# A fused attention and feed-forward block: a weight load moved to ScalarE's queue, another held back, and new instruction orders

## The chip, the cores and the metric

The kernel runs on one core of a Trainium2 chip. The metric is device time in microseconds (us) of one launch; the median of three runs before the change is 183.61 us (183.45 to 183.64). Engines: TensorE (PE in the profile, with its weight loads as PEld), VectorE (DVE), ScalarE (ACT), GpSimd (POOL) and SyncE (SP). Before the change every transfer is issued from SP's queue.

## The reference

With `xn = layernorm(x)` for 2048 rows of 512 features, the result is `x + A(xn) + B(xn)`, all in bf16:

```python
qkv = (xn @ wqkv)                      # 512 -> 3 x 512, 32 heads of 16
# A: row s attends to rows s, s-2, ..., s-14 (8 offsets), masked below row 0
logits = einsum("bhsd,bhswd->bhsw", q, k[idx]) / 4
A = (softmax(logits) @ v[idx]) @ wo    # 512 -> 512
# B: gated feed-forward
B = (gelu(xn @ w_gate) * (xn @ w_up)) @ w_down   # 512 -> 1376 -> 512
```

## The kernel before, in words

**Tiling.** The rows are cut into four blocks b = 0 to 3 of 512 rows, sixteen tiles of 128. For each block the kernel normalizes the rows, brings them into transposed form `xnT`, makes q, k and v, the eight logits of each head, a softmax, the weighted sum of v, the feed-forward products, and one output product that adds both branches in the same PSUM bank. The blocks overlap: while VectorE is at the attention of one block, TensorE is at the feed-forward of the same or the next.

**Tasks and names.** Each piece of work is a named task of one engine, with the line on which its instruction stands in the profile of before. The name ends in the block, and after that in the part; `fu0_3` is the fourth up-projection of block 0. For block 0 and the head of the program the last number is a tile.

- TensorE: `warm` (L637, products of constants while x is on its way), `tpx0_t`, `tpy0_t` (L883, the two halves of the transpose of tile t = 0, 1), `tpx1_t` (L872, tiles 2 and 3), `mma0_t`, `mmb0_t` (L961, q of tile t from the first and the second half of the features), `mmt0_t`, `mmt1_t` (L947, q of tiles 2, 3 and k of all four), `mmv` (L1005, v of block 0), `fg`, `fu` (L1250, gate and up; part 10 on L1289), `mmB_w_g_0` (L1030, q, k, v for w = 0, 1, 2 of blocks 1 to 3), `er` (L1097 the last piece of the up-projection, then L1104 the sum over a head's features), `acca`, `accb`, `accd`, `accw` (L1342, the output product).
- VectorE: `bnst`, `bnag`, `sub`, `rstd`, `norm` (L712 to L842, layernorm of tiles 0 to 7; `rstd8` to `rstd14` on L765), `mean1`, `evy0_t` (L897, half of a transposed tile out of PSUM), `pr` (L1061, q times eight shifted k), `pa`, `pb` (L1073, L1080, sums of these), `mask` (L1127), `d1`, `d2` (L1138, L1145, the maximum and its subtraction), `d4` (L1164), `d6` (L1182), `pv` (L1212, weights times shifted v), `pw`, `pz` (L1221 to L1232, their sums), `h` (L1274, L1312, gate times up), `fin` (L1380, L1386, adding x).
- ScalarE: `c_tbl` (L627, a one-element square root that brings in its table), `sx1`, `negm1`, `sxx1`, `sq` (L722 to L768, the statistics of tile 1 and the square roots), `evx0_t`, `evx1_t` (L905), `evq`, `evk`, `evv` (L983, L1015, L1041), `gelu`, `uev` (L1260, L1267), `bnst8` to `15`, `bnag8` to `15`, `sub8` to `15`, `norm8` to `15` (the layernorm of the later tiles), `ve`, `vp`, `va` (L762), `vb` (L790), `lc` (L1133), `exp`, `ln`, `d5` (L1156, L1174, L1178), `halo`, `halv` (L1049), `fe` (L1375).
- GpSimd: constants, and `sq8`, `sq10`, `sq12`, `sq14` (L794, a power of one half of two columns, between `vb` and `rstd`).
- SP's queue: `ld_x` (L693, L699), `ld_wq`, `ld_wk`, `ld_wv` (L646), `ld_wg0`, `ld_wu0` (L655), `ld_wt` (L662), `ld_wd` (L667, L671), `ld_wo` (L674), `trx` (L855, transposes of tiles 4 to 15 into `xnT`, two numbers: pair of tiles and tile of the pair), `ss` and `sl` (L1191, L1204, the softmax weights through memory and back, spread), `ldxr` (L1327, x again for `fin`), `sto` (L1393, the result).

**What sets the order.** The table `ORDER` holds, written out, one list of task names for each engine, and every engine runs its list strictly in turn. `Graph.schedule` walks the five lists with a table of costs (durations, `nbytes` for a load) to see which buffer slot each task gets; the same walk gives `assign_sync` the waits: a task waits for the semaphores of what it depends on. So the costs in the tasks do not move an instruction past another on its engine; they can only change which slot is taken and which wait is found to be covered by an earlier one. A list entry with `on_act` set is issued by ScalarE's queue, ahead of all of ScalarE's own tasks.

**Buffers around the change.** `XIN` has four slots for pairs of tiles of x. In the order of before x0, x1, x2 and x4 take the four; `ld_x3` stands behind them, and waits for the slot of x0, which is free when `tpy0_1` has read tile 1. `ld_wg0` depends on `ld_wk` having landed. `XR` has two slots for `ldxr0` to `ldxr7`; a third load waits for the `fin` of an earlier one. `xnT` of a block is complete when its four `trx` have landed, and the block's `mm` wait for all four.

Of the kernel before, what the change touches and what calls it, by code (L numbers as in the profile page):

```python
# [96 lines left out]
class Graph:  # L97
# [225 lines left out]
    def emit_engine(self, eng_name, e):  # L323
        if eng_name == "act":
            for t in self.order["sp"]:
                if t.on_act:
                    assert not t.waits
                    ins = t.emit(e)
                    ins.then_inc(t.sem, 16)
                    t.ins_name = ins.ins.name  # L330
# [17 lines left out]
    def report(self):  # L348
# [17 lines left out]
        "warm13 warm14 mma0_0 tpx0_1 tpy0_1 mmb0_0 mma0_1 mmb0_1 mmt1_0 tpx1_0 mmt1_1 mmt0_2 tpx1_1 mmt1_2 "  # L366
        "mmv0_1 mmt0_3 mmt1_3 mmv0_0 mmv1_0 fg0_0 fg0_1 fg0_2 fg0_3 fu0_0 fu0_1 fu0_2 fu0_3 fg0_4 mm1_0_0_0 "
        "fu0_4 mm1_1_0_0 fg0_5 mm1_1_1_0 fu0_5 er0_3 mm1_0_1_0 fg0_6 mm1_2_3_0 fg1_0 mm1_0_2_0 mm1_1_2_0 "
        "mm1_0_3_0 mm1_1_3_0 fu1_0 fg0_7 fu0_6 fu0_7 fg1_1 fu1_1 fg0_10 fg0_8 fg1_2 fu1_2 fg1_3 mm1_2_2_0 "
        "fu1_3 fg0_9 fg1_4 mmv1_1 fu1_4 fu0_8 fu0_9 er1_3 fg1_5 mm1_2_0_0 fg1_6 fu1_5 fg1_7 fg1_8 fu1_6 fg1_9 "  # L370
        "fu1_7 mm2_1_0_0 mm2_0_0_0 mm2_1_3_0 fu1_8 mm2_1_1_0 mm2_0_2_0 fg2_0 mm2_0_1_0 mm1_2_1_0 mm2_0_3_0 "
        "fu2_0 mm2_1_2_0 fg1_10 accd3 fu1_9 fg2_1 fu2_1 fg2_2 fg2_3 fg2_4 mm2_2_2_0 acca0 fu2_2 accb0 fg2_5 "
        "accd1 fg2_10 er2_3 fg2_6 mm2_2_3_0 mm2_2_1_0 mm2_2_0_0 mm3_0_2_0 mm3_0_3_0 fu2_3 fu2_4 mm3_1_1_0 "
        "mm3_1_2_0 fu2_5 accd2 mm3_0_0_0 mm3_1_3_0 fg3_0 mm3_1_0_0 fu2_6 fg3_1 fu3_0 fg2_7 fu3_1 fg3_2 "
        "mm3_0_1_0 fg3_3 mm3_2_2_0 fu3_2 mm3_2_0_0 acca4 fu3_3 fu2_7 accd7 accd5 er3_3 fg2_8 accb4 fg3_4 "
        "fg3_5 fg2_9 fu2_8 mm3_2_1_0 accd6 fg3_6 mm3_2_3_0 fu3_4 fu3_5 fg3_7 fg3_8 fu2_9 fg3_10 fu3_6 fu3_7 "
        "fg3_9 fu3_8 fu3_9 acca8 accb8 accd11 acca12 accd15_1 accd9 accb12 accd13 accd14_0 accd10 accd15_0 "
        "accw13 accw15_1 accw15_0 accw12 accd14_1 accw14_0 accw14_1 accd15_2 accw15_2",
    "act":
        "c_tbl sx1 sq0 negm1 sxx1 sq1 evx0_0 evx0_1 sq2 evq0_0 evq0_1 evx1_0 sq3 evk0_0 evk0_1 bnst8 evx1_1 "  # L380
        "bnst9 sq4 evk0_2 ve8 sq6 evq0_2 vp8 evq0_3 evk0_3 bnag8 evv0_0_1 bnag9 evv0_1_0 sub9 gelu0_0 bnst10 "
        "bnst11 uev0_0 va8 gelu0_3 gelu0_1 ve10 gelu0_2 vp10 evv0_0_0 uev0_3 vb8 evq1_0_0 bnag10 evk1_0_0 "
        "uev0_4 uev0_2 bnag11 uev0_1 va10 halo1 bnst12 evk1_1_0 vb10 lc0 evq1_1_0 uev0_5 gelu0_5 gelu0_6 "
        "gelu0_4 exp0 evq1_2_0 evv1_3_0 evq1_3_0 bnst13 evk1_3_0 ln0 d5_0 evk1_2_0 gelu1_0 sub10 uev0_6 "
        "gelu1_1 uev1_1 uev1_0 sub8 uev0_10c ve12 uev0_10a uev0_10b uev0_7 norm8 gelu0_10 gelu0_8 sub11 "
        "gelu0_7 evv1_2_0 gelu1_3 gelu1_2 vp12 uev1_2 evv0_1_1 uev1_3 gelu1_4 norm11 uev0_9 uev0_8 lc1 bnag12 "
        "norm10 gelu0_9 norm9 gelu1_6 uev1_4 bnag13 evv1_0_0 uev1_5 bnst14 gelu1_7 uev1_6 gelu1_5 bnst15 "
        "uev1_7 gelu1_8 gelu1_9 exp1 evk2_1_0 uev1_8 evq2_0_0 va12 ve14 evk2_0_0 halo2 vb12 sub13 vp14 halv1 "
        "evv1_1_0 evq2_1_0 evk2_3_0 bnag14 uev1_10b sub12 ln1 d5_1 uev1_10c evk2_2_0 evq2_3_0 uev1_10a "
# [48 lines left out]
def bass_parallel_sum__sliding_local_dilated__glu_gated_geglu__prompt_kernel(nc, A_x, A_wqkv, A_wo, B_x, B_w_gate, B_w_up, B_w_down, out, dbg=None, cfg=None):  # L438
# [43 lines left out]
    with contextlib.ExitStack() as es:  # L482
# [61 lines left out]
        G = Graph()  # L544
# [912 lines left out]
```

## Time and profile before

| | us |
|---|---|
| median of three runs (range) | 183.61 (183.45 to 183.64) |
| the profiled execution | 183.42 |
| its span, first to last instruction | 181.3 |
| PE, DVE, ACT, POOL busy | 176.5, 168.7, 131.7, 18.5 |
| first `warm` product, first transpose, first product with Wq | 0.83, 4.93, 5.94 |
| first gate product `fg0_0` | 16.74 |
| last product ends | 178.98 |

The timeline gives start and duration of an instruction or of a run of like ones; the second figure of a run of matmuls contains the modelled drain of the last, so that runs overlap by some 0.17 us. The step from one start to the next is the time that a task takes of the stream. `SPq` is the issue of a transfer on SP's queue. The waits view sums the idle time of an engine by what ended it. What lies between the span and the profiled time (2.1 us) is before the first and after the last instruction.

### The profile page before, as it was taken

How to read it: one execution, taken by the hardware profiler on the slowest of the kernel's cores; microseconds unless marked ns; L12 is line 12 of the kernel's file. 1: busy time of each engine (PE TensorE's matmuls, PEld its weight loads, DVE VectorE, ACT ScalarE, POOL GpSimd, SP SyncE). 2: the span in 40 equal slices, each digit the busy share in tenths (PEclk: the TensorE clock that was granted, in tenths of full speed). 3: DMA queues.
4: the chain of work that ended last, by engine and by line, in shares of the span. 5: the costliest groups of instructions: out<-in, count | busy, mean ns of one | idle time of the engine just before them, and what ended most of it. 6: DMA issues, size and time to landing. Idle time of an engine off the chain costs nothing.

```text
span 181.3 us, 2762 instructions
## 1 busy us (share of the span) xinstructions
PE 176.5 (97%) x1043; PEld 90.7 (50%) x1060; DVE 168.7 (93%) x157; ACT 131.7 (73%) x270; POOL 18.5 (10%) x23
## 2 busy tenths in 40 slices
PE   8999999999999999999999999999999999999994
PEld 2897444544454455444445444444444444454574
DVE  3989996899999999989999999999999999999953
ACT  5689999999999999999297599835177679411030
POOL 6000035200000002954000000000000000000000
PEclk9999999999999999999999999999999999999999
DMA  4999984002792200002671000518004057410113
GB/s 130 357 379 386 156 218 162 2 0 58 161 329 56 58 4 0 0 0 66 168 206 29 0 0 0 140 61 266 29 0 147 3 120 226 146 58 4 58 47 98
DMA packets 26220, 19.60 MB, mean 108 GB/s; under 512 B 13824, under 2 KB 23008, under 8 KB 26208
## 3 DMA queue, kind: packets, MB, share of 16 engines
q1 hardware_dynamic: 26208, 19.44, 38.1%
q8 instruction: 8, 0.13, 0.3%
q14 instruction: 4, 0.03, 0.1%
HBM read 14.71 MB, written 3.15 MB: 98 GB/s over the span
## 4 chain that ended last, share of the span: by engine, by line
DVE 54%; ACT 21%; PE 10%; POOL 5%; DMA 5%; issue 4%; SPq 1%; DVEq 0%
DVE UNI L1212 14%; DVE UNI L1061 9%; DVE UNI L1221 7%; POOL sq L794 5%; ACT GG L1260 4%; DVE UNI L1073 4%; ACT UU L1267 4%; DVE UNI L1227 4%; DVE HT L1274 3%; DMA XIN<-in_A_x_dram 3%; PE PS L1342 3%; PE PS L637 2%; DVE OT L1232 2%; DVE OB L1380 2%; DMA xnT<-XIN 2%
## 5 line engine op out<-in xcount | busy, mean ns | idle before, releaser
L1342 PE MATMUL PS<-Wd,HT 128*128 128x512 bf16 (+2 forms) x206 | 40.5, 345 | 0.2
L1250 PE MATMUL PS<-xnT,Wu 128*128 128x512 bf16 x156 | 38.9, 379 | 0.2
L1250 PE MATMUL PS<-xnT,Wg 128*128 128x512 bf16 x155 | 38.7, 379 | 0.4 <-issue 0.2
L1212 DVE TENSOR_TENSOR UNI<-VN,PT 128x8192 f16<-128x8192 bf16 x8 | 35.4, 4420 | 0.0
L1061 DVE TENSOR_TENSOR UNI<-QT,KT 128x8192 f16<-128x8192 bf16 x8 | 35.3, 4420 | 0.0
L1030 PE MATMUL PS<-xnT,Wqkv 128*128 128x512 bf16 x142 | 34.5, 380 | 0.3
L1342 PEld LDWEIGHTS PS<-Wd,HT 128*128 128x128 bf16 x209 | 19.7, 98 | 19.4
L1267 ACT ACTIVATE UU<-PS 128x512 bf16<-128x512 f32 x40 | 23.2, 608 | 6.0 <-PE PS L1250 5.9
L1375 ACT ACTIVATE OB<-PS 128x512 bf16<-128x512 f32 x14 | 8.3, 595 | 23.2 <-PE PS L1342 23.1
L1250 PEld LDWEIGHTS PS<-xnT,Wu 128*128 128x128 bf16 x160 | 15.6, 98 | 18.6 <-ACT KT L1041 0.3
L1250 PEld LDWEIGHTS PS<-xnT,Wg 128*128 128x128 bf16 x160 | 15.1, 98 | 19.4 <-ACT UU L1267 0.8
L1030 PEld LDWEIGHTS PS<-xnT,Wqkv 128*128 128x128 bf16 x144 | 16.1, 114 | 16.0 <-DMA xnT<-XIN 0.6
L1260 ACT ACTIVATE GG<-PS 128x512 bf16<-128x512 f32 x40 | 22.9, 609 | 0.5 <-DVE HT L1274 0.4
L794 POOL TENSOR_TENSOR sq<-ve,mhalf 128x2 bf16<-128x2 f32 x4 | 15.7, 3916 | 65.8 <-ACT ve L790 65.8
L1221 DVE TENSOR_TENSOR UNI<-UNI 128x8192 f16<-128x8192 f16 x4 | 17.7, 4422 | 0.0
L1073 DVE TENSOR_TENSOR UNI<-UNI 128x8192 f16<-128x8192 f16 x4 | 17.7, 4421 | 0.0
L1342 PE MATMUL PS<-Wo,OT 128*128 128x512 bf16 (+2 forms) x75 | 16.1, 345 | 0.1
L1274 DVE TENSOR_TENSOR HT<-GG,UU 128x1024 bf16<-128x1024 bf16 x20 | 13.5, 685 | 0.0
L1342 PEld LDWEIGHTS PS<-Wo,OT 128*128 128x128 bf16 x76 | 6.9, 98 | 6.4 <-DVE OT L1232 0.5
L1227 DVE TENSOR_TENSOR UNI<-UNI 128x4096 f16<-128x4096 f16 x4 | 9.1, 2286 | 0.0
L1041 ACT ACTIVATE KT<-PS 128x512 bf16<-128x512 f32 x12 | 7.2, 600 | 2.4 <-PE PS L1030 2.4
L1041 ACT ACTIVATE VN<-PS 128x512 bf16<-128x512 f32 x12 | 7.2, 598 | 1.0 <-PE PS L1030 0.9
(99 smaller groups left out, 180.3 us busy)
## 6 DMA issues: line engine op xcount, KB each, us to landing
PT<-pt_scratch SPq DMA_DIRECT2D x16, 256.0 KB, 4.3
out_dram<-OB SPq DMA_DIRECT2D x14, 128.0 KB, 1.8
XIN<-in_A_x_dram SPq DMA_DIRECT2D x12, 128.0 KB, 2.6
Wqkv<-in_A_wqkv_dram SPq DMA_DIRECT2D x3, 512.0 KB, 5.0
XIN<-in_A_x_dram SPq DMA_DIRECT2D x6, 256.0 KB, 5.8
Wg<-in_B_w_gate_dram SPq DMA_DIRECT2D x1, 1280.0 KB, 8.7
Wu<-in_B_w_up_dram SPq DMA_DIRECT2D x1, 1280.0 KB, 11.6
Wd<-in_B_w_down_dram SPq DMA_DIRECT2D x1, 1280.0 KB, 7.7
```

Of the source, the lines that this page charges most:

```text
L794: "pool", "sq%d" % t, 5.0, lambda e, t=t, n=n: e.tensor_tensor(out=sq[:, t:t + n], in0=ve[:, t:t + n], in1=mhalf[:, 0:n], op=ALU.pow),
L1030: ins = e.matmul(PS[:, 512 * it.slot:512 * it.slot + 512], lhsT=wcols(which, kt, g), rhs=xnT[:, itx.slot, kt, :], start=(kt == 0), stop=(k ...
L1061: return lambda e: e.tensor_tensor(out=UNI[:, it.slot:it.slot + 2, :, :], in0=bass.AP(QT, (itq.slot * 4 + 2 * h) * 512, [[NQT * 4 * 512, 1 ...
L1073: return lambda e: e.tensor_tensor(out=UNI[:, i0.slot:i0.slot + 2, :, :], in0=UNI[:, i0.slot:i0.slot + 2, :, :], in1=UNI[:, i1.slot:i1.slo ...
L1212: return lambda e: e.tensor_tensor(out=bass.AP(UNI, ito.slot * 4096, [[NUNI * 4096, 128], [2048, 4], [512, 4], [1, 512]]), in0=bass.AP(VN, ...
L1221: return lambda e: e.tensor_tensor(out=UNI[:, i0.slot:i0.slot + 2, :, :], in0=UNI[:, i0.slot:i0.slot + 2, :, :], in1=UNI[:, i1.slot:i1.slo ...
L1227: return lambda e: e.tensor_tensor(out=UNI[:, i0.slot, :, :], in0=UNI[:, i0.slot, :, :], in1=UNI[:, i0.slot + 1, :, :], op=ALU.add)
L1250: ins = e.matmul(PS[0:M, 512 * it.slot:512 * it.slot + 512], lhsT=Wx[:, kt, j * 128:j * 128 + M], rhs=xnT[:, itx.slot, kt, :], start=(kt = ...
L1260: return lambda e: e.activation(out=GG[:, ito.slot, q, :], in_=PS[:, 512 * it.slot:512 * it.slot + 512], func=ACTF.Gelu_apprx_tanh)
L1267: return lambda e: e.activation(out=UU[:, ito.slot, q, :], in_=PS[:, 512 * it.slot:512 * it.slot + 512], func=ACTF.Identity)
L1274: return lambda e: e.tensor_tensor(out=HT[:, ito.slot, j - 1:j + 1, :], in0=GG[:, ig.slot, :, :], in1=UU[:, iu.slot, :, :], op=ALU.mult)
L1342: ins = e.matmul(PS[:, 512 * it.slot:512 * it.slot + CW], lhsT=(OT[:, ito.slot, q, ti * 128:(ti + 1) * 128] if kind == "o" else HT[:, ith. ...
```

## The change

Three pieces, and new lists for four engines (GpSimd's stays).

1. `ld_wq` is issued by ScalarE's queue, ahead of `c_tbl`. It gets a wait: it reads the tile that VectorE's first task `c_wdz` (a fill of part of Wd, L620) writes, so that ScalarE waits for `c_wdz`, then issues the transfer, then loads its table. In SP's list the place of `ld_wq` issues nothing.
2. `ld_wk` gets a wait for the landing of `ld_x0_0`, the first 128 rows of x. SP's queue stands until then.
3. The lists change. On TensorE `mmb0_0` comes ahead of the transposes of tile 1, and `mma0_1`, `mmb0_1` come later. On VectorE `bnst2` and `bnag2` come between the pieces of tile 1. The rest of all four lists is another order of the same tasks.

The costs of the planner change for `c_tbl`, `ld_wq`, `ld_wg0`, `ld_wu0`, `ld_wt`, `ld_wo`; no instruction's own work does.

```diff
         if eng_name == "act":
             for t in self.order["sp"]:
                 if t.on_act:
-                    assert not t.waits
+                    for (s, v) in t.waits:
+                        e.wait_ge(s, v)
                     ins = t.emit(e)
...
     "pe":
-        "warm13 warm14 mma0_0 tpx0_1 tpy0_1 mmb0_0 mma0_1 mmb0_1 mmt1_0 tpx1_0 mmt1_1 mmt0_2 tpx1_1 mmt1_2 "
-        "mmv0_1 mmt0_3 mmt1_3 mmv0_0 mmv1_0 fg0_0 fg0_1 fg0_2 fg0_3 fu0_0 fu0_1 fu0_2 fu0_3 fg0_4 mm1_0_0_0 "
-        "fu0_4 mm1_1_0_0 fg0_5 mm1_1_1_0 fu0_5 er0_3 mm1_0_1_0 fg0_6 mm1_2_3_0 fg1_0 mm1_0_2_0 mm1_1_2_0 "
...
-        "fg3_9 fu3_8 fu3_9 acca8 accb8 accd11 acca12 accd15_1 accd9 accb12 accd13 accd14_0 accd10 accd15_0 "
-        "accw13 accw15_1 accw15_0 accw12 accd14_1 accw14_0 accw14_1 accd15_2 accw15_2",
+        "warm13 warm14 mma0_0 mmb0_0 tpx0_1 tpy0_1 mmt1_0 tpx1_0 mmt1_1 mmt0_2 tpx1_1 mma0_1 mmb0_1 mmt1_2 "
+        "mmt0_3 mmt1_3 mmv0_0 mmv1_0 mmv0_1 fg0_0 fg0_1 fg0_2 fg0_3 fu0_0 fu0_1 fu0_2 fu0_3 fg0_4 mm1_1_1_0 "
+        "mm1_0_1_0 mm1_1_2_0 fg0_5 mm1_0_0_0 er0_3 mm1_1_0_0 fu0_4 fg0_6 fg1_0 fg1_1 fu0_5 mm1_0_2_0 "
...
+        "fg3_9 fu2_9 fu3_8 fu3_9 acca8 accb8 acca12 accb12 accd15_0 accd9 accd14_0 accd15_1 accd10 accd11 "
+        "accd13 accw15_1 accw15_0 accw12 accw13 accw14_0 accd14_1 accw14_1 accd15_2 accw15_2",
     "dve":
-        "c_wdz bnst0 bnag0 sub0 rstd0 norm0a norm0b mean1 sub1 evy0_0 rstd1 norm1a norm1b bnst2 bnag2 evy0_1 "
...
-        "rstd4 sub6 sub7 rstd6 norm4 norm7 sub5 norm6 norm5 pr0_0 pr0_1 pa0 h0_1 mask h0_0 rstd8 d1a_0 d1b_0 "
...
-        "h0_4 d1b_1 pv0_0 d1c_1 h1_2 d2_1 h1_3 pw0_1 d4a_1 pw0_2 d4b_1 pz0 d4c_1 pr2_0 rstd12 d6_1 pr2_1 "
+        "c_wdz bnst0 bnag0 sub0 rstd0 norm0a norm0b mean1 bnst2 sub1 evy0_0 rstd1 bnag2 norm1a norm1b sub2 "
...
+        "rstd4 sub5 sub6 sub7 rstd6 norm4 norm5 norm6 norm7 pr0_1 pr0_0 pa0 rstd8 h0_0 mask h0_1 d1a_0 d1b_0 "
...
+        "h0_4 d1b_1 pv0_1 d1c_1 d2_1 h1_2 pw0_1 rstd12 d4a_1 pw0_2 d4b_1 h1_3 d4c_1 pz0 pr2_1 h1_4 d6_1 pr2_0 "
+        "fin3 pa2 rstd14 pb2 h1_10 pv1_0 d1a_2 d1b_2 d1c_2 fin0 d2_2 pv1_1 d4a_2 d4b_2 h2_0 d4c_2 h2_1 fin1 "
...
     "sp":
-        "ld_x0_0 ld_x0_1 ld_wq ld_x1_0 ld_wk ld_x1_1 ld_wv ld_x2 ld_x4 ld_x3 ld_wg0 ld_wu0 ld_x5 trx3_1 "
-        "ld_wt0 trx3_0 ld_wt1 ld_wt2 trx2_1 trx2_0 ld_x6 ld_wd0 ss0_0 ss0_3 ss0_1 ss0_2 ld_wd1 ld_x7 sl0_3 "
...
+        "ld_x0_0 ld_x0_1 ld_x1_0 ld_wq ld_wk ld_x1_1 ld_x2 ld_wv ld_x4 ld_x3 ld_wg0 ld_wu0 ld_x5 ld_wt0 "
+        "trx3_0 ld_wt1 trx3_1 trx2_1 trx2_0 ld_x6 ld_wt2 ld_wd0 ld_x7 ss0_3 ss0_1 ldxr3 ss0_2 ss0_0 sl0_0 "
...
+        "sl1_0 trx6_1 ldxr2 sl1_2 trx7_1 trx7_0 ldxr1 ldxr9 trx6_0 ss2_3 ss2_1 ss2_0 ldxr4 sto1 ldxr7 ldxr10 "
...
-        G.task("act", "c_tbl", 1.3, lambda e: e.activation(
+        G.task("act", "c_tbl", 1.75, lambda e: e.activation(
...
-                         prio=(-958, -957.5, -898)[i], nbytes=(900 if i == 0 else 512) * 1024)
+                         prio=(-958, -957.5, -898)[i], nbytes=(450 if i == 0 else 512) * 1024,
+                         rd=[(I_wd, 2)] if i == 0 else [])
+            if i == 0:
+                t_w.on_act = True
+                t_w.dur = 0.01
             t_ld["w" + nm] = t_w
...
-            t_w = G.task("sp", "ld_w%s0" % nm, 0, mk(), wr=[I_w], prio=R_WG + (nm == "u"), nbytes=1280 * 1024)
+            t_w = G.task("sp", "ld_w%s0" % nm, 0, mk(), wr=[I_w], prio=R_WG + (nm == "u"), nbytes=(1540 if nm == "g" else 1180) * 1024)
...
+            t_w.dur = (0.57, 0.93, 0.93)[i]
...
+        t_w.dur = 1.13
...
+                    if p + t2 == 0:
+                        t_ld["wk"].deps.add(t_x)
```

## The prediction

> **What bounds the kernel now.** I read the page first, then TensorE's timeline, the chain's end, the waits, and the timelines of the other engines at the places that these named. The page:
>
> ```profile
> span 181.3 us, 2762 instructions
> ...
> PE 176.5 (97%) x1043; PEld 90.7 (50%) x1060; DVE 168.7 (93%) x157; ACT 131.7 (73%) x270; POOL 18.5 (10%) x23
> ```
>
> PE and DVE are both nearly full, so neither share says which ends last. The chain of waits, at its end:
>
> ```profile
> 172.02 1.20 DVE OT L1232
> 173.23 0.04 issue
> 173.27 0.44 DVE OB L1380
> 173.73 5.26 PE PS L1342 x49
> ```
>
> `pz3`, the last attention result, is there at 173.22. TensorE's first product that needs it starts at 173.73: it was busy with other output products until then. So at the end TensorE is late, by some 0.5 us, not VectorE. Its timeline tells where it lost time:
>
> ```profile
> 23.43 1.03 PE L1250 MATMUL PS<-xnT,Wg 128*128 128x512 bf16 x4
> 24.58 1.05 PE L1030 MATMUL PS<-xnT,Wqkv 128*128 128x512 bf16 x4
> ...
> 93.74 0.62 PE L1097 MATMUL PS<-xnT,Wt 128*32 128x256 bf16 x16 [0.43 <-ACT UU L1267]
> ```
>
> Four products of 512 columns step by 0.86 us (26.33 to 27.20, say). From 23.43 to 24.58 is 1.15: 0.29 lost at the first `mm1`. In the same way 0.25 is lost before 47.99 (`mm1_2_2_0`), 0.43 before 93.74 (`er2_3`), 0.20 before 152.79 (`acca8`): 1.17 in all, in 173 us from 5.94 (`mma0_0`) to 178.98. The new lists hold the same products, so 1.2 us and the little that the head gives is the most that they can gain; the 2.3 us from the last product to the span's end and the 2.1 us around it stay. VectorE must keep up; its waits:
>
> ```profile
> DVE PS L1127 <- PE PS L1104: 1.7, 1, 1.7
> ...
> DVE rstd L765 <- POOL sq L794: 0.6, 1, 0.6
> ```
>
> **What the Trainium skill says.** "DMA: Bandwidth & Descriptors", section "Issuing engines are not separate DMA queues": transfers of different issuing engines run on the same 16 DMA engines and interleave; a second issuer saves only issue time. Before, everything goes over one queue, so no run yet shows it. "GPSIMD Engine Reference", section "Specifications": GpSimd's SBUF interfaces are shared with VectorE, with contention where a VectorE instruction has two SBUF inputs. The trace agrees: the same two-column power took 1.18 to 8.30 us:
>
> ```profile
> 31.74 1.18 POOL L794 TENSOR_TENSOR sq<-ve,mhalf 128x2 bf16<-128x2 f32 x1 [2.01 <-ACT ve L790]
> 71.33 8.30 POOL L794 TENSOR_TENSOR sq<-ve,mhalf 128x2 bf16<-128x2 f32 x1 [38.41 <-ACT ve L790]
> ```
>
> The short one met a pause of VectorE (idle 0.4 before 32.86). The long one lay under two-input instructions back to back, and ended at 79.63, 0.55 after `pr2_0` ended at 79.08.
>
> **Part by part.** *Wq on ScalarE's queue.* `c_wdz` ends at 1.18; an issue on SP took 0.43; ScalarE's is in no trace, I take 0.43 (range 0 to 0.9). Then the table load (1.28) and the square root (0.20 with its start), so `c_tbl` ends near 1.2 + 0.43 + 1.28 + 0.20 = 3.1, and `sx1` starts at 3.44, on x's second tile: hidden by 0.3; at 0.9 it would cost 0.2. Wq starts 0.5 earlier than SP's 1.71. The first load on SP was issued at 0.80 and landed 2.1 later, the second 2.2, Wq 4.1, Wk 5.0 (the view of issues, cut to each). Wq now interleaves with x's second tile (landed at 3.42), and that tile holds `sx1`, `sq0` behind it on ScalarE, `rstd0`, the first transpose and `mma0_0`. 128 KB take 0.42 at the later rate (Wk's landing to Wv's, 7.73 to 9.85, for 640 KB); at half of it, 0.4 more. Cost 0 to 0.4 on the path; I take 0.1.
>
> *Wk held.* SP's next issue would come at 2.2, and stands until 2.95. Behind it wait `ld_x1_1`, x2, Wv, x4, x3, Wg and Wu; Wk's issue moves from 2.73 to about 3.0, each of these 0.25 later. Their cover is the backlog: x1_0 and Wq, 640 KB, 2.1 us at that rate. Before, the DMA engines were little used from 3 to 4.3 us[...]; with Wq ahead I expect everything after it 0.5 earlier (0 to 0.7): Wk 7.2, x3 11.6, Wg 16.0, Wu 19.3 (before 7.73, 12.10, 16.47, 19.78). x3 still waits for `tpy0_1`, now near 7.3 rather than 6.8; with 1.5 MB queued ahead of it that is covered. `ld_wg0` still waits for Wk.
>
> *The head.* `bnst2` (0.6 net) stands ahead of `sub1` and `evy0_0`, so `evy0_0` ends near 6.45 rather than 5.86. `mma0_0` runs 5.94 to 6.38: `mmb0_0` loses 0.1, the transposes of tile 1 another 0.2 (`norm1b` at 7.1), then `mmt1_0` waits for Wk, 0.0 to 0.4. After it 6 x 0.89 for `mmt`, 0.45 for two transposes, 0.89 for `mma0_1`, `mmb0_1`, 3 x 0.87 for `mmv`: 9.3, and `fg0_0` at 16.6 to 17.0; before 16.74. I take 16.75, no gain.
>
> *VectorE's start.* All three `mmv` now follow `mmt1_3`; before one came ahead, so `evk0_3` ends 0.8 earlier than 15.84. The norms take 3.8 from `bnst6` (12.13, on x3) to `pr`; with x3 at 11.6, `pr` starts at 15.4 rather than 15.95. `er0_3` stands 14 rather than 15 tasks behind `fg0_0` and no longer behind a wait: its end at 30.3 rather than 31.37, so `mask` comes 1.1 earlier, and VectorE's 1.7 of idling becomes 0.8. `rstd8` ahead of it is hidden in that.
>
> *SP's queue.* `ld_wt0` (0.57) is issued before the first `trx` in time that SP stood idle, `ld_wt2` (0.93) after the last. `trx3_0` waits for `norm6`, 0.2 later than `norm7` was at 15.11. The last `trx` of block 1 is issued 0.9 to 1.2 earlier, and lands near 23.5, not 24.53; TensorE wants it at 24.5: the 0.29 is gone. Later, `ldxr1` stands ahead of `trx6_0` and waits for the `XR` slot that `fin0` frees. `fin0` comes after `d1c_2`, near 97.6; two issues of 0.6, 1.3 for `trx6_0` and 1.4 to land make 101.5, and `mm3_0_0_0` is due near 101.6. Margin nothing, cost 0 to 0.5.
>
> *The long middle.* The places of the other three waits (0.25, 0.43, 0.20) changed; what stands there now has other inputs, and I can't see its waits in this trace. The bound below is 0, the bound above what the old list lost in all, 1.2; I take 0.5, for `er2_3` against `pb2` (both near 92), `trx6_0`, `acca8` against `pz2` (near 152). `rstd12` moves from behind `pr2_0` to behind `pw0_1`, before `d4a_1`; its `vb12` moves by 7 us of ScalarE's work, to about 63.5. The power ends 0.55 after `pw0_1` does (69.1), as it did after `pr2_0`: 0.6 for VectorE, as before. `rstd14` may cost 0.6 after `pa2` (before nothing).
>
> *VectorE's sum* to `pz3`: 173.25 - 0.55 (start) - 0.85 (`mask`) + 0.6 (`rstd14`) = 172.45 at the latest of the known. TensorE's last attention products fall due at 173.73 - 0.6 = 173.1: it still bounds. The nine tasks after `pz3` are the same ones, 5.26.
>
> **The sum**, against the profiled 183.42: +0.1 (x's second tile), 0 (head), -0.29 (first `mm1`), -0.88 (three old waits), +0.5 (new ones) = -0.57: 182.85. The median stood 0.19 above the profile; of the order of the spread of the runs, so I take half: 182.95.
>
> **Rivals.** *Full gain:* no new waits, x's second tile on time: 183.5 - 1.2 = 182.3. For it, DVE runs about 0.8 ahead of before throughout; against it, the thin margins above. *The gain is eaten:* the second tile late by 0.4, new waits of 1.0 in place of 1.17: -0.3 + 0.5, so 183.6 within 0.4. It includes the case that Wq on the other queue is no earlier, and x3 stays at 12.1: VectorE then starts at 15.95, and `er2_3` waits for `pb2`. *Slower, by the power:* if `sq12`'s 8.30 us is its length wherever it runs, it ends at 63.5 + 8.3 = 71.8, and `rstd12`, due at 69.1, holds VectorE 2.6 rather than 0.6. Then `pb2` is 2.0 later, and `er2_3` holds TensorE for nearly all of it: 182.95 + 1.8 = 184.75. It decides from a wait of about 1.2 on, the power ending after 70.3. Against it, 1.18 and 2.01 for the same work elsewhere.
>
> **How the numbers follow.** Forecast (182.5 to 183.3) 0.48, full gain 0.18, eaten 0.19, slower 0.15. The likeliest is 182.95. The forecast's own range is 182.5 to 183.3; the wide one leaves out a tenth at either end: from 182.1 (full gain with a better head) to 184.5. Faster by over 0.2% (0.37 us, about what a measurement can tell from no change), below 183.24, holds the full gain and nearly all of the forecast: 0.65. Same, to 183.98: 0.19. Slower: 0.16.
>
> **What would show it.** Right: the first `pr` at 15.3 to 15.6, the first `mm1` with no step over 0.9, `mask` near 30.5, `rstd12` waiting about 0.6, the last product ending at 178.2 to 178.6. Wrong: `sx1` later than 3.6 (interleaving), `pr` at 15.9 (no earlier loads), more than 1.2 of new waits on TensorE, a `rstd` held for over a us, or TensorE idle for `pz3` before the last 5.26.

## The result: slower by 1.3%

| | before | changed |
|---|---|---|
| median of six runs (range), us | 183.53 (183.37 to 184.34) | 186.31 (184.20 to 186.77) |
| profiled execution, its span | 183.42, 181.3 | 186.59, 184.5 |
| `sx1` starts (second tile of x there) | 3.44 | 5.62 |
| first gate product `fg0_0` starts | 16.67 | 20.11 |
| last product ends | 178.98 | 182.15 |

The ratio is 1.0132, with a 95% interval of 1.0082 to 1.0181. I had forecast 182.95, and faster: wrong in sign. Five of the six runs lie between 186.1 and 186.8, and one took 184.20; that gap is part of the answer. Four of the five had a mean granted TensorE clock of 0.991, which stands for one stretch at half speed, shown below; the run of 186.14 and that of 184.20 had 1.00. (Every run has this figure, also one without a profile; below, "a half-speed stretch on record" means 0.991.)

All of the loss is at the start. `fg0_0` comes 3.44 late, the last product 3.17. (Its start is taken here as the end of the product before it. In the timeline it is 0.16 earlier, 19.95 in the changed kernel; the 16.74 of before is the second of its products, as the record of the first is missing.)

In the page of the changed kernel, TensorE (PE) is as full as it was, and still ends last. Two things are new: the first digits of `PEclk` are no longer all 9, and there is a second queue, q10, ScalarE's.

```profile
span 184.5 us, 2781 instructions
...
PE 178.8 (97%) x1060; PEld 92.1 (50%) x1060; DVE 168.6 (91%) x157; ACT 131.9 (71%) x270; POOL 15.6 (8%) x23
...
PEclk9879999999999999999999999999999999999999
...
q10 hardware_dynamic: 528, 0.52, 1.2%
```

The chain of work that ended last (start, duration, what) begins with a piece that was not worth a thought before: the second tile of x, 4.34 us on its way. It ends, as before, in TensorE's output products; there is no wait for `pz3` (on OT, ended at 176.06; the product that needs it started at 176.7).

```profile
1.26 4.34 DMA XIN<-in_A_x_dram
...
156.13 26.03 PE PS L1351 x165
```

The view of issues, cut to the time in which that tile is issued, before and after: it landed 2.2 us after its issue, now 4.3. Wq, which takes the other queue, took 4.1 and now 4.9.

```profile
XIN<-in_A_x_dram SPq DMA_DIRECT2D x1, 128.0 KB, 2.2
```

```profile
Wqkv<-in_A_wqkv_dram ACTq DMA_DIRECT2D x1, 512.0 KB, 4.9
XIN<-in_A_x_dram SPq DMA_DIRECT2D x1, 128.0 KB, 4.3
```

ScalarE's timeline (start, duration, then what it is, and in brackets the idle time before it and what ended that) shows who suffers. The issue of Wq and the table load are over at 2.98 as foreseen, and hidden. `sx1` (L731) then waits 2.43 for the tile; and everything up to the first transpose hangs on it.

```profile
1.21 0.45 ACTq L647 DMA_DIRECT2D Wqkv<-in_A_wqkv_dram  x1
1.70 1.28 ACT L628 ACT_TABLE_LOAD   x1 [1.70 <-DVE Wd L621]
2.99 0.20 ACT L628 ACTIVATE onef<-onef 128x1 f32<-128x1 f32 x1
5.62 0.63 ACT L731 ACTIVATE XR<-XIN 128x512 bf16<-128x512 bf16 x1 [2.43 <-DMA XIN<-in_A_x_dram]
```

TensorE has warmed up by 4.81 and stands until 7.11. What comes then runs at half speed: in the view by stretches (busy time of each engine in a stretch; the third number from the end is the granted clock), 7.2 to 11.0 has a mean of 0.59. The single records give 0.50 from 7.92 to 11.33, that is for 3.41 us.

```profile
7.11 0.48 PE L892 MATMUL PS<-ident,XIN 128*128 128x128 bf16 x4 [2.31 <-DVE XIN L851]
```

```profile
4.80:7.20 2.40, 0.09 (x2) 0.10 (x2) 0.60 (x4) 1.54 (x5) 0.00 (x0) 1.00 1.02 347
7.20:11.00 3.80, 3.80 (x39) 3.55 (x39) 3.21 (x14) 1.97 (x7) 0.00 (x0) 0.59 0.96 312
```

Before, TensorE was busy for 2.36 of the 2.40 us from 4.8 to 7.2, and no half-speed stretch followed:

```profile
4.80:7.20 2.40, 2.36 (x32) 1.92 (x31) 2.24 (x11) 1.44 (x5) 0.00 (x0) 1.00 1.08 361
7.20:11.00 3.80, 3.80 (x70) 3.80 (x70) 2.94 (x11) 2.98 (x7) 0.00 (x0) 1.00 1.09 353
```

The view says 1.00 also where the trace has no clock record. In both kernels TensorE begins at half speed: the warming products of 512 columns step by 0.43 us there, later products of that width by 0.22. The record of full clock begins at 5.58 before, and at 4.50 in the changed kernel, 3.41 before its half-speed stretch.

The waits that I had read off the timeline of before are gone at two of the places shown there: the first `mm1` starts 0.86 after the gate product, and `er2_3` (L1106) has no idle time noted. VectorE's wait at `mask` is 1.3 instead of 1.7.

```profile
26.86 1.03 PE L1259 MATMUL PS<-xnT,Wg 128*128 128x512 bf16 x4
27.72 1.67 PE L1039 MATMUL PS<-xnT,Wqkv 128*128 128x512 bf16 x7
...
94.95 0.62 PE L1106 MATMUL PS<-xnT,Wt 128*32 128x256 bf16 x16
```

```profile
DVE PS L1136 <- PE PS L1113: 1.3, 1, 1.3
```

So there were two suspects, the queue and the clock, and against them the rest of the change: the hold on Wk, and the new orders of the head.

### The profile page after: what moved, and what is told of

It is laid out like the page before. It is cut to its first block, busy times and chain, and to the rows that moved or that the text cites. A ratio compares the mean times of both kernels' runs of the same rounds, so it can differ in the third digit from the quotient of the medians.

```text
span 184.5 us, 2781 instructions
## 1 busy us (share of the span) xinstructions
PE 178.8 (97%) x1060; PEld 92.1 (50%) x1060; DVE 168.6 (91%) x157; ACT 131.9 (71%) x270; POOL 15.6 (8%) x23
## 4 chain that ended last, share of the span: by engine, by line
DVE 33%; PE 32%; issue 14%; ACT 12%; POOLq 4%; DMA 2%; POOL 1%; SPq 0%; DVEq 0%
PE PS L1351 14%; DVE UNI L1221 11%; PE PS L1259 8%; DVE UNI L1082 5%; DVE UNI L1070 5%; POOLq L483 4%; PE PS L956 3%; PE PS L1039 2%; ACT GG L1269 2%; DMA XIN<-in_A_x_dram 2%; DVE UNI L1230 2%; DVE HT L1283 2%; ACT UU L1276 2%; PE PS L970 2%; PE PS L1014 1%
## 5 line engine op out<-in xcount | busy, mean ns | idle before, releaser
L1269 ACT ACTIVATE GG<-PS 128x512 bf16<-128x512 f32 x40 | 23.4, 606 | 3.2 <-PE PS L1259 2.4
L1259 PEld LDWEIGHTS PS<-xnT,Wu 128*128 128x128 bf16 x160 | 15.4, 98 | 19.4 <-ACT KT L1050 0.5
L803 POOL TENSOR_TENSOR sq<-ve,mhalf 128x2 bf16<-128x2 f32 x4 | 12.7, 3177 | 75.8 <-ACT ve L799 75.8
```

What stands on the lines that cost most here:

```text
L803: "pool", "sq%d" % t, 5.0, lambda e, t=t, n=n: e.tensor_tensor(out=sq[:, t:t + n], in0=ve[:, t:t + n], in1=mhalf[:, 0:n], op=ALU.pow),
L1259: ins = e.matmul(PS[0:M, 512 * it.slot:512 * it.slot + 512], lhsT=Wx[:, kt, j * 128:j * 128 + M], rhs=xnT[:, itx.slot, kt, :], start=(kt = ...
L1269: return lambda e: e.activation(out=GG[:, ito.slot, q, :], in_=PS[:, 512 * it.slot:512 * it.slot + 512], func=ACTF.Gelu_apprx_tanh)
```

## The experiments

Ratios are to runs of the kernel before on the same chip, with 95% intervals; times are medians.

**1. Wq back on SyncE's queue.** All else as changed.

```diff
-                         rd=[(I_wd, 2)] if i == 0 else [])
-            if i == 0:
-                t_w.on_act = True
+                         rd=[])
 # SP's list
-        "ld_x0_0 ld_x0_1 ld_x1_0 ld_wq ld_wk ...
+        "ld_x0_0 ld_x0_1 ld_wq ld_x1_0 ld_wk ...
```

> The changed kernel with one part undone: Wq is issued by SyncE's queue again, behind the second tile of x. The hold on Wk, the head's order and all other orders stay as changed. Theory A (Wq on ScalarE's queue takes the DMA engines from x's second tile, 5.60 instead of 3.42 us; everything in the head is late by that and by the half-speed TensorE clock that follows): the second tile lands at 3.4 to 3.6, no half-speed stretch after 7.9 us, and the time is 182.9 (182.3 to 183.4), below the kernel before by what the new order gains. Theory B (the loss is in the head's new order or in the hold on Wk): the time stays at 185.5 to 186.5.

Measured 184.21, ratio 1.0050 (1.0035 to 1.0066). The tile landed at 3.42 and the half-speed stretch is gone: 1.9 of the 2.78 us were that. But 0.87 stays, where I had expected a gain. The profile says where: on VectorE `bnst2` (L718) waits for x1_0 until 6.40, and `sub1` and `evy0_0` stand behind it; TensorE's `mmb0_0` (L967) then waits for `evy0_0`. VectorE's timeline, then TensorE's:

```profile
6.40 0.69 DVE L718 BATCH_NORM_STATS2 st<-XIN 128x6 f32<-128x512 bf16 x1 [1.27 <-DMA XIN<-in_A_x_dram]
```

```profile
7.60 0.64 PE L967 MATMUL PS<-xnT,Wqkv 128*128 128x128 bf16 x8 [0.84 <-DVE xnT L903]
```

**2. Wq on ScalarE's queue alone**, in the kernel before, with its orders and no hold.

```diff
-                         prio=(-958, -957.5, -898)[i], nbytes=(900 if i == 0 else 512) * 1024)
+                         prio=(-958, -957.5, -898)[i], nbytes=(450 if i == 0 else 512) * 1024,
+                         rd=[(I_wd, 2)] if i == 0 else [])
+            if i == 0:
+                t_w.on_act = True
```

> The kernel before with one part of the change alone: Wq is issued by ScalarE's queue ahead of its table load, waiting for the cleared tile c_wdz; all orders are as before, and Wk is not held. Theory A: the second tile of x lands at about 5.5, TensorE is idle for over 2 us and then runs at half clock for 3 to 4 us, and the time is 186 (185.5 to 187), as for the whole change or a little above it. Theory B: the time is within 0.4 of the kernel before.

Measured 183.44, ratio 1.0000 (0.9988 to 1.0012), twelve runs, none above 183.64. The tile landed at 3.80. So the queue alone does not do it, and the theory in its plain form fell. The tile in the view of issues:

```profile
XIN<-in_A_x_dram SPq DMA_DIRECT2D x1, 128.0 KB, 2.5
```

**3. More warming products** in the changed kernel: eleven more of 512 columns ahead of the first transpose.

```diff
-        WARM = cfg.get("WARM", ([512] * 9 + [128], [128] * 5))
+        WARM = cfg.get("WARM", ([512] * 20 + [128], [128] * 5))
```

> The changed kernel with eleven more of the 512-column warming products ahead of the first transpose, so that TensorE is busy in what was its idle time of 2.3 us (4.81 to 7.11). Nothing else is changed: the second tile of x is still late. Theory A1 (the half-speed clock from 7.92 to 11.33 follows from that idle time and costs 1 to 1.6 us of its own): the half-speed stretch is gone and the time is 184.7 to 185.3. Theory A2 (half clock is hidden by ScalarE's and VectorE's steps in the head, so only the 2.2 us of the transfer count): 186.0 to 186.6, no change.

Measured 185.79 (four runs, 185.17 to 186.51), between both forecasts. The tile was late (5.51). This trace has no clock record, but the products show full speed: after the wait for the tile, 128 columns step by 56 ns, against 107 ns in the half-speed stretch of the changed kernel. `fg0_0` came 1.07 earlier than in the changed kernel; but the edit had moved something else. The planner gives PSUM banks by its own estimate of time, and 145 of the 191 results in PSUM have another bank. `er1_3` got a bank that `uev0_9` had to empty first, and in TensorE's timeline that is a new wait:

```profile
58.30 0.62 PE L1105 MATMUL PS<-xnT,Wt 128*32 128x256 bf16 x16 [1.33 <-ACT UU L1275]
```

Run 11 repeats it with the banks kept. In runs 1, 2, 4 to 9 and 13 every task has the bank that it has in the kernel they start from.

**4. No hold on Wk**, the rest as changed.

```diff
-                    if p + t2 == 0:
-                        t_ld["wk"].deps.add(t_x)
```

> The changed kernel without the hold: Wk is issued as soon as SyncE's queue reaches it, no longer waiting for the first tile of x. Theory A: no help for the second tile, since Wk stands behind it; within 0.4 of the changed kernel's 186.3, or up to 1 us worse if Wk adds to what the second tile shares. Theory B in the form that the hold is to blame (everything behind it on the queue late): back to 183.0 to 183.6.

Measured 184.25, ratio 1.0045 (1.0028 to 1.0061). Both forecasts missed. The tile landed at 3.86 in the profiled run, and the time is that of the first experiment; but one of the four runs took 187.40 (left out of the interval), and its cause is not known.

**5. Queue and hold together**, in the kernel before, orders kept: if it takes both, this has both.

```diff
 # as the second experiment, and
+                    if p + t2 == 0:
+                        t_ld["wk"].deps.add(t_x)
```

> The kernel before, all its orders kept, with the two edits on transfers alone: Wq issued by ScalarE's queue and Wk held until the first tile of x has landed. Wq on ScalarE's queue alone cost nothing (second tile of x at 3.80), and the hold alone, with Wq on SyncE's queue, left that tile at 3.42; only with both was it at 5.5 to 5.6. Theory C (it takes both: with SyncE's queue silent from 2.2 to 3.0, Wq's packets start before those of x's second tile are through): second tile at 5.4 to 5.7 in most runs, and 185.3 to 186.3. Theory D (it was the new orders, or chance): second tile at 3.4 to 3.9, within 0.4 of the kernel before.

Measured 183.59, ratio 1.0011 (0.9999 to 1.0023), 21 runs, of which 19 lie below 184. Tile at 3.50. The theory that it takes both fell as well, though up to 2.1 us the engines are given the same work here as in the changed kernel.

**6. Wk one place later** in the changed kernel: x1_1 is issued while SP's queue stood still.

```diff
-        "ld_x0_0 ld_x0_1 ld_x1_0 ld_wq ld_wk ld_x1_1 ...
+        "ld_x0_0 ld_x0_1 ld_x1_0 ld_wq ld_x1_1 ld_wk ...
```

> The changed kernel with one pair exchanged on SyncE's queue: x1_1 is issued ahead of the held Wk and so at 2.2 to 2.7, when the changed kernel's queue stood still; Wk waits as before. Theory C1 (any further issue on SyncE's queue at that moment lets x's second tile through ahead of Wq): second tile at 3.4 to 3.9, time 184.0 to 184.7. Theory C2 (only an unheld Wk does it, by what it puts into the queue): second tile at 5.4 to 5.7, 186.0 to 186.8.

Measured 185.06, eight runs from 184.04 to 187.46 (ratio 1.0083, 1.0052 to 1.0113). Neither forecast: four runs at 184.0 to 184.7, like the first experiment, two at 186.2 and 186.6, like the changed kernel, and one each at 185.4 and 187.5 (the last left out of the ratio). The two at 186.2 and 186.6 have a half-speed stretch on record, the others none. The profiled run (186.17) has the tile at 5.50. The same program seems to fall on either side.

So I looked at the records of the two issues in nanoseconds, and at the first packets. In the changed kernel the issue of the second tile on SP and that of Wq on ScalarE end within 10 ns of each other:

| kernel | Wq's issue ends, ns | tile's issue ends, ns | Wq's first packet, us | tile lands, us |
|---|---|---|---|---|
| 3, more warming | 1664 | 1673 | 2.35 | 5.51 |
| changed | 1665 | 1674 | 2.40 | 5.60 |
| 6, Wk one later | 1667 | 1674 | 2.43 | 5.50 |
| 4, no hold | 1670 | 1671 | 2.76 | 3.86 |
| 2, queue alone | 1675 | 1667 | 2.77 | 3.80 |
| 5, queue and hold | 1680 | 1663 | 2.77 | 3.50 |

Where Wq was 7 to 9 ns ahead, its packets began at 2.4 and the tile was late; where the tile was ahead, or they were 1 ns apart, they began at 2.77 and the tile was in time. The tile's own first packet tells the same (of 1 KB, one row; taken as the 129th of SP's queue, as each tile has 128): in the lower three it began at 2.47 to 2.49, ahead of any of Wq's; in the upper three at 3.38 to 3.57, after 92 to 101 of Wq's. That looks like a race, and a race can be decided by hand.

**7. Wq a little later**: ScalarE waits also for `c_vnpad`, done at 1.48.

```diff
                 t_w.on_act = True
+                t_w.deps.add([t for t in G.tasks if t.name == "c_vnpad"][0])
```

> The changed kernel, with Wq on ScalarE's queue and Wk held, but ScalarE waits also for GpSimd's c_vnpad (done at 1.48) before it issues Wq, so that this issue runs from 1.5 to 1.95 instead of 1.21 to 1.67. Theory R (a race: in the kernels whose second tile of x was late, the issue of Wq ended 7 to 9 ns before that of the second tile, at 1.674; in those whose tile was in time it ended 1 ns before to 17 ns after; whoever is first gets its packets through first): now Wq is always second, the second tile lands at 3.4 to 3.9 in every run, and the time is 184.2 (183.9 to 184.5) with no run near 186. Rival (Wq on another queue together with the hold makes the tile late, whatever the order of issue): second tile at 5.4 to 5.7, 186.0 to 186.6.

**8. Wq a little earlier**, in the kernel of the second experiment, which had lost nothing: it waits for `c_onef` (1.04) in place of `c_wdz` (1.19).

```diff
-                         rd=[(I_wd, 2)] if i == 0 else [])
+                         rd=[(I_onef, 0)] if i == 0 else [])
```

> The kernel before, with all its orders and no hold, and Wq on ScalarE's queue as in the second experiment, but waiting for GpSimd's c_onef (done at 1.04) instead of c_wdz (1.19): this issue runs from 1.06 to 1.5, and so ends ahead of that of the second tile of x (1.67) in every run. Theory R: second tile at 5.2 to 5.7, TensorE idle for 2 us before the first transpose, 185.3 to 186.6. Rival (it takes the hold, or the new orders): second tile at 3.4 to 3.9, 183.2 to 183.7.

Wq's issue in the timeline, of the later, then of the earlier one:

```profile
1.56 0.46 ACTq L647 DMA_DIRECT2D Wqkv<-in_A_wqkv_dram  x1
```

```profile
1.07 0.46 ACTq L647 DMA_DIRECT2D Wqkv<-in_A_wqkv_dram  x1
```

And the second tile of x in the view of issues, its time from issue to landing last, in the same order:

```profile
XIN<-in_A_x_dram SPq DMA_DIRECT2D x1, 128.0 KB, 2.2
```

```profile
XIN<-in_A_x_dram SPq DMA_DIRECT2D x1, 128.0 KB, 4.2
```

Later: tile at 3.45, and 184.50 over nine runs (ratio 1.0060, 1.0036 to 1.0084). Eight lie from 183.96 to 185.03; one took 186.06, which the forecast excluded; it has no profile, but a half-speed stretch on record. In the profiled run (185.03) Wk landed only at 9.01, and TensorE waited 1.2 us for it. Earlier: tile at 5.45, 186.52 (1.0145, 1.0113 to 1.0177); five of six runs at 186.46 to 186.95, in a kernel with none of the new orders and no hold. Issuing Wq 0.14 us earlier moved that kernel by 2.9 us, each time against its own runs of before. So the race is shown from both sides: in the profiled runs by the tile's landing, in the others by the times, with one exception on each side (186.06 and 184.91).

**9. VectorE's `bnst2` back behind `sub1`**, in the kernel of the first experiment, for the 0.87 that was left.

```diff
-... mean1 bnst2 sub1 evy0_0 rstd1 bnag2 norm1a norm1b sub2 ...
+... mean1 sub1 evy0_0 rstd1 norm1a norm1b bnst2 bnag2 sub2 ...
```

> The changed kernel with Wq back on SyncE's queue (184.21 in the first experiment) and in addition VectorE's bnst2 and bnag2 back behind sub1, evy0_0, rstd1 and norm1a/b. TensorE's new order is kept. Theory E (bnst2 waits for x1_0 until 6.4 and holds sub1, evy0_0 and so mmb0_0 behind it, a gap of 1.03 on TensorE): evy0_0 ends at 5.9 again, the gap ahead of mmb0_0 is under 0.2, but mmt1_0 then waits for Wk (landed at 7.9) as mma0_1 and mmb0_1 no longer stand ahead of it, so fg0_0 starts at 17.2 instead of 17.8, and the time is 183.6 (183.3 to 183.9). Theory F (it is TensorE's order that costs, whatever VectorE does): 184.0 to 184.4.

Measured 184.15 (1.0036, 1.0022 to 1.0050): no gain, the rival's value. The wait for `evy0_0` is gone, and TensorE now waits for Wk (landed at 8.21) ahead of `mmt1_0`, with `mma0_1` and `mmb0_1` no longer in front of it to fill the time. What follows `mmt1_0` starts at 9.18, against 9.21 with the wait in the other place:

```profile
8.26 1.08 PE L953 MATMUL PS<-xnT,Wqkv 128*128 128x128 bf16 x16 [0.59 <-DMA Wqkv<-in_A_wqkv_dram]
```

**10. The old head, the new rest**: the lists of before up to `fg0_0`, the new ones after it; Wq on SP, no hold. Run twice, the second time with the PSUM banks of the later tasks set by hand so that they pass from task to task as in the changed kernel.

```diff
-... mma0_0 mmb0_0 tpx0_1 tpy0_1 mmt1_0 ... tpx1_1 mma0_1 mmb0_1 mmt1_2 ... fg0_0
+... mma0_0 tpx0_1 tpy0_1 mmb0_0 mma0_1 mmb0_1 mmt1_0 ... fg0_0
 # second run
+                if it.psum and it.name in PS_SLOT:
+                    k0 = PS_SLOT[it.name]
+                    at = dict((k, f) for k, f in at.items() if k0 <= k < k0 + it.width)
```

> The orders of the kernel before up to the first product of the gate (up to norm5 on VectorE, evk0_3 on ScalarE, the load of x5 on SyncE's queue), then the new orders; Wq on SyncE's queue, no hold. If the new order of the rest is worth what the gaps of TensorE after fg0_0 say (1.77 against 2.05 us), 183.1 (182.8 to 183.3), below the kernel before; the rival, that the rest gains nothing once it starts on time: 183.3 to 183.8.

> As the run with the orders of before up to the first product of the gate and the new orders after that (Wq on SyncE's queue, no hold), but with the PSUM banks of the later tasks set by hand so that they pass from task to task as in the changed kernel: in the run without that, the planner gave er0_3 banks that waited for evk1_2_0, and TensorE stood 1.8 us. Theory H (the changed kernel's loss without the race is its head, 1.0 to 1.1 us at fg0_0; its later orders gain about 0.3): fg0_0 at 16.8, no wait ahead of er0_3, and 183.1 (182.8 to 183.4). Rival (the later orders need the late head to have their inputs there): a new wait of 0.5 or more, 183.6 to 184.2.

Measured 185.13 (1.0096, 1.0081 to 1.0110) and 183.88 (1.0024, 1.0009 to 1.0039). `fg0_0` started at 16.84 and 17.00: the old head lists give back 0.8 to 1.0 us. But in both, TensorE then waits at `er0_3`. In the first its banks came from `evk1_2_0`, which ended as the wait did; in the second they are right, and the wait ended with `pa0` (29.58), on which `er0_3` depends; the view calls it `issue`.

```profile
30.64 0.62 PE L1101 MATMUL PS<-xnT,Wt 128*32 128x256 bf16 x16 [1.65 <-ACT KT L1045]
```

```profile
29.68 0.62 PE L1122 MATMUL PS<-xnT,Wt 128*32 128x256 bf16 x16 [0.60 <-issue]
```

So the rival is right: in the new order `er0_3` stands one task nearer to `fg0_0`, and that costs nothing only if TensorE is late. One of the 22 runs of the second took 186.18, with a half-speed stretch on record though Wq is on SP's queue.

**11. More warming products, banks kept.**

```diff
 # as the third experiment, and the banks of the changed kernel in PS_SLOT
```

> The changed kernel with eleven more of the 512-column warming products, as in the third experiment, but with the PSUM banks of all later tasks kept as in the changed kernel (there the planner gave er1_3 other banks, and it stood 1.5 us). The second tile of x will be late in most runs. Theory A1 (the half-speed clock after TensorE's idle time costs 1.1 us of its own): 185.2 (184.9 to 185.5) in those runs, no half-speed stretch. Theory A2 (half clock is hidden): 186.0 to 186.6.

Measured 185.54, five runs from 185.34 to 186.05; 0.77 below the changed kernel's 186.31, above the 185.2 forecast. The tile was late (5.68). Wq's issue had ended at 1.659, 8 ns ahead of the tile's. The clock was full from 6.25 on, and stayed so (until then the added products step by 0.43 us, and the 1.00 of the first line is not a record):

```profile
4.80:7.20 2.40, 2.40 (x10) 0.87 (x8) 0.52 (x3) 1.46 (x5) 0.00 (x0) 1.00 1.07 355
7.20:11.00 3.80, 3.73 (x56) 3.19 (x55) 3.50 (x14) 2.10 (x7) 0.00 (x0) 1.00 0.93 298
```

The added products themselves held the first transpose until 7.9, where the changed kernel had it at 7.1, so between the two profiled runs (185.78 and 186.59) the half clock cost at least the 0.8 that they differ by. But the changed kernel's own run without a half-speed stretch on record took 186.14, only 0.13 to 0.63 less than the four with one. It has no profile, and three kept traces (3, 7 and 13) show that a record can be missing. So the price of the half clock is not settled.

**12. `bnst2` first, alone**, in the kernel before (the banks of the later tasks kept by hand).

```diff
-... mean1 sub1 evy0_0 rstd1 norm1a norm1b bnst2 bnag2 ...
+... mean1 bnst2 sub1 evy0_0 rstd1 norm1a norm1b bnag2 ...
```

> The kernel before with one task moved: VectorE's bnst2 ahead of sub1 (the PSUM banks of the later tasks kept as before). Theory (the edit costs by itself): bnst2 waits for x1_0 until 6.4, sub1 starts at 7.0 instead of 5.2, norm1b ends at 8.1 instead of 6.5, the transposes of tile 1 and mma0_1, mmb0_1 behind them are 1.5 later, fg0_0 starts at 18.2 instead of 16.7, and the wait of 0.3 ahead of the first product of block 1 goes: 184.7 (184.4 to 185.1). Rival (TensorE waits for Wk in any case, which hides it): 183.4 to 183.9.

Measured 184.98 (1.0106, 1.0055 to 1.0156), as forecast: the edit costs by itself. Four of the six runs lie from 184.24 (the profiled one, tile at 3.33) to 185.01. The two at 186.56 and 186.59 have a half-speed stretch on record, again with Wq on SP's queue: so it doesn't take the second queue to bring it on. `bnst2` waits for x1_0, and TensorE for `norm1` ahead of the transposes of tile 1 (VectorE's timeline, then TensorE's):

```profile
5.97 0.69 DVE L733 BATCH_NORM_STATS2 st<-XIN 128x6 f32<-128x512 bf16 x1 [0.93 <-DMA XIN<-in_A_x_dram]
```

```profile
7.57 0.48 PE L904 MATMUL PS<-ident,XIN 128*128 128x128 bf16 x4 [1.08 <-DVE XIN L863]
```

**13. `ld_wt2` later, alone**, in the kernel before: one load behind `trx2_1`, `trx2_0` and `ld_x6` on SP.

```diff
-... ld_wt1 ld_wt2 trx2_1 trx2_0 ld_x6 ...
+... ld_wt1 trx2_1 trx2_0 ld_x6 ld_wt2 ...
```

> The kernel before with one load moved on SyncE's queue: ld_wt2 behind the last transposing transfers of block 1 (trx2_1, trx2_0) and ld_x6 instead of ahead of them; nothing else. If that is what the first product of block 1 waits for, trx2_0 lands at 23.5 to 24.2 instead of 24.5, the 0.3 ahead of mm1_0_0_0 is gone, and the time is 0.2 to 0.35 below the kernel before. Rival (the transfers wait for their data, not for the queue, or the time goes to the next wait): within 0.15 of the kernel before.

Measured 183.31 against 183.54, ratio 0.9983 (0.9967 to 0.9999), 22 runs. `trx2_0` landed at 24.11 instead of 24.53, and the step from the gate product to the first product of block 1 is 0.87 instead of 1.15. This is the only edit of the change that was seen to gain, and the only version here that beats both kernels, by a margin close to what can be measured.

```profile
23.52 1.03 PE L1250 MATMUL PS<-xnT,Wg 128*128 128x512 bf16 x4
24.39 1.03 PE L1030 MATMUL PS<-xnT,Wqkv 128*128 128x512 bf16 x4
```

## Where the prediction went wrong

Three pieces make up the 2.78 us, each as the difference of two medians above their own runs of before: the new orders 0.87 (first experiment), the late tile 1.12 more (185.54 is 1.99 above 183.55), the half clock the last 0.79. The split of the last two is rough, for the reasons given under 11. Most of the 0.87 is the head's: with the old head and the same banks 0.33 is left (10), though there at a new wait.

*Wq on ScalarE's queue*: the step that failed. I wrote that Wq interleaves with the tile, and priced that at "0 to 0.4 on the path; I take 0.1", from 128 KB at half of the later rate. It was 2.2 us at the tile. Sharing as such was priced right: where the tile was first (2 and 4), it landed at 3.80 and 3.86, 0.4 late, and in 2 the kernel lost nothing. What failed is that the tile could come second: from 2.75 to 3.5 only Wq's packets moved in the changed kernel, 50 of 1 KB each in 0.75 us, at 120 to 380 ns a packet on average, and the tile's began at 3.57. Before, Wq had a slow start too, a milder one (12 KB from 3.0 to 3.25, then 41 to 63 KB in each quarter of a microsecond up to 4.25), but behind the tile, where it cost nothing. I saw that the two would share the engines, and did not ask who would be first. The sign I named ("`sx1` later than 3.6") appeared. The issue time itself (0.43 guessed, 0.45 measured) and the cover of the table load (3.1 guessed, 3.19 measured) were right.

I had quoted the Trainium skill, "DMA: Bandwidth & Descriptors", section "Issuing engines are not separate DMA queues", for the statement that a second issuer saves only issue time. The runs agree that it gains nothing (1.0000 in the second experiment). They add that it can cost. The same page's section "Queues, rings and completion order" says that an engine takes turns between the rings of queues at the grain of packets, and that a packet is typically 9 to 17 descriptors, so a turn is more than one row of 1 KB, if a row is one descriptor. The trace does not contradict that: 94 of Wq's rows had begun before the tile's first, an estimated 6 for each of the page's 16 engines, less than one such turn; and from 3.75 to 5.25 both queues moved side by side. Which engine moved which row is not in the trace, so that Wq's first turn held up the tile is not shown.

*The clock* was in no step. The same skill, "TensorE: Matmul & The Clock Gate", "Part 1: The HAM clock gate", has TensorE at half clock after an idle window of about 3.4 us, until about 3.4 us of work. The stretch at half speed was 3.41 us here, which agrees; the idle time ahead of it was only 2.31 us, shorter than what the page names. When it comes after an idle time differs: the record has full clock for 3.41 us and then half clock, from 7.92 in the changed kernel, 6.96 in 6 and 8.89 in 8, while TensorE restarts at 7.11, 7.01 and 6.96. The price was missing: a wait of 2 us on TensorE need not be over when it ends.

*Wk held*: no loss was seen (1.0000 without and 1.0011 with it in 2 and 5; 184.25 without and 184.21 with it in 4 and 1, where Wq's queue differs too). But Wk landed at 8.62 in 5 and at 7.64 in 2, and in 7 and 9, where TensorE waited 1.23 and 0.59 for it, the hold was in place; its share there is open. The gain behind it, every later load 0.5 earlier, did not come. x3 landed at 12.85 and Wg at 18.18, for 11.6 and 16.0 foreseen: they are late with the tile. In the first experiment, with the tile in time, x3 landed at 11.99, 0.1 earlier than before, and only Wg came clearly earlier (15.35 for 16.47).

*The head*, "no gain": wrong by 0.9. I let `evy0_0` end near 6.45, with 0.6 for `bnst2`, as if its input lay ready. It waits for x1_0, which had landed at 6.12 in the trace of before, the one that I used; `evy0_0` ends at 7.54 in the first experiment. I also allowed 0.0 to 0.4 for the wait for Wk. It was 0.59 once `bnst2` was out of the way. With the one or the other, TensorE is past `mmt1_0` within 0.03 of the same time, which is why removing one showed nothing.

*VectorE's start* follows the head: the first `pr` at 18.46 for 15.4, `mask` at 33.67 for 30.5.

*SP's queue*: that the first `mm1` loses its wait is right, and the thirteenth experiment shows that the load order alone removes it. In the changed kernel the late start would have done so too, as the next point shows. That `ldxr1` ahead of `trx6_0` would be just in time is right: `trx6_0` landed at 104.17, and its product started at 105.0 without a wait.

*The middle and the sum.* -0.29 and -0.88 against +0.5 should have left 0.67. From `fg0_0` to the end of its last product TensorE took 0.27 less than before. But the eighth experiment has the old orders and a head just as late (`fg0_0` 0.11 later than in the changed kernel), and its last product ends 0.09 later: the same length within 0.02. The first `mm1` waits for nothing there either: its inputs are there when TensorE comes late. TensorE's timeline of that run, where products of 512 columns step by 0.86 to 0.87 across it:

```profile
26.97 1.03 PE L1255 MATMUL PS<-xnT,Wg 128*128 128x512 bf16 x4
27.84 1.03 PE L1035 MATMUL PS<-xnT,Wqkv 128*128 128x512 bf16 x4
28.70 1.03 PE L1255 MATMUL PS<-xnT,Wu 128*128 128x512 bf16 x4
```

So what I first took for a gain of the new orders, the 0.27, the old orders give back as well when they start late. New waits of about 0.7 in all replaced the old ones, at `fu1_9`, `mm2_2_0_0` and `mm3_2_3_0`.

*The power.* The rival in which `sq12` holds VectorE was wrong (and its 2.6 should read 2.7, 71.8 less 69.1): `sq12` took 0.99, and `rstd12` did not wait. `rstd14` after `pa2` waited 0.6, as I wrote it might. GpSimd's timeline and a line of the waits (total, times, longest):

```profile
67.13 0.99 POOL L803 TENSOR_TENSOR sq<-ve,mhalf 128x2 bf16<-128x2 f32 x1 [29.80 <-ACT ve L799]
84.89 7.47 POOL L803 TENSOR_TENSOR sq<-ve,mhalf 128x2 bf16<-128x2 f32 x1 [16.76 <-ACT ve L799]
```

```profile
DVE rstd L774 <- POOL sq L803: 0.6, 1, 0.6
```

*Left open.* What shifts the two issues by some nanoseconds from kernel to kernel, and from run to run, was not found. Of runs without a profile it is not known whether their tile was late: the 184.20 of the changed kernel is what its other parts cost, and so fits, but that is argued only. A half-speed stretch on record does not tell it either, as single runs with Wq on SP's queue had one (10, 12, and 185.60 in a run of the kernel before). Why Wq's first packets are slow was not tried.

## What to carry to other kernels

When a large load moves to a second queue, ask which small transfer it meets at the DMA engines, and which of the two issues ends first; if the margin is some nanoseconds, make one wait for something, or leave it on the one queue, where the tile landed at 3.3 to 3.5 in all seven traces here. Before moving a task ahead on an in-order engine, look up when its input lands, not only how long it runs, and move only what has its input. And price TensorE's idle time at the start with the half-speed stretch that can follow it; and check what a new order gains against an old order that starts equally late.

## What the runs showed of the hardware

- Two transfers were issued on SP's and ScalarE's queues. Where the issue of the 512 KB load ended 7 to 9 ns or more ahead of that of a 128 KB tile (five traces), the tile landed at 5.4 to 5.7 us; where it ended 1 ns ahead or later (four traces), at 3.4 to 3.9 us.
- TensorE stood for 2.3, 2.7 and 2.0 us near the start (changed kernel, 6 and 8) and was then granted half the clock for 3.41 us, from 0.8 us after its restart, from 0.05 us ahead of it, and from 1.9 us after it. Products of 128 columns stepped by 107 ns in it, by 56 ns outside. With the wait filled by products (11) the half clock did not come.
- At the start of the kernel TensorE ran at half speed (512 columns in 0.43 us, later in 0.22), until 3.55 us in 6, 4.50 in the changed kernel, 5.58 before and 6.25 in 11.
- While the 512 KB load began in the changed kernel, with rows of 1 KB on ScalarE's queue, the engines moved 14 to 18 KB in each quarter of a microsecond from 2.75 to 3.5 us, against 84 to 96 KB over both queues from 4.0 to 5.0 us.
- The same power of two columns on GpSimd took 0.99 and 7.47 us in one execution.
